# A one-token decode block rewritten on one core: 512-column score matmuls, row-form softmax and LayerNorm, a finer split of the last weight load

## The chip, the cores and the metric

One core of one Trainium2 (trn2) chip. The metric is the device time of one execution in microseconds (us), as the median of several runs. The span that a profile shows is about 1.8 us shorter than the device time of the same execution, so spans are compared with spans and times with times.

In this document PE is the tensor engine, PEld its weight loads, DVE the vector engine, ACT the scalar engine, POOL the GpSimd engine, and SP the sync engine, which issues all loads on one queue. The profile counts 16 DMA engines. PV is the product of the softmax weights with V, LN2 the second LayerNorm. A load lands at the last of the times that the trace has for it, 16 for every load but the small one of x. h2T, aT, hT and yT are small buffers of the kernels.

## The reference

One token goes through attention over the last 1024 cached positions and then through a GELU-gated feed-forward block, each behind a LayerNorm.

```python
# x: (1, 1, 640); 32 heads of 128; k_cache, v_cache: (1, 32, 4096, 128), last W = 1024 rows used
h  = x + attention(layernorm(x)) @ wo     # q = layernorm(x) @ wq, softmax(q k^T / sqrt(128)) v
h2 = h + (gelu(layernorm(h) @ w_gate) * (layernorm(h) @ w_up)) @ w_down    # F = 1728
```

All inputs are bf16. The core must read K and V (8.4 MB each), wq and wo (5.2 MB each) and w_gate, w_up and w_down (2.2 MB each), 33.9 MB in all, for a single row of activations.

## The kernel before

Every buffer is large enough to be loaded whole, so the sync engine issues the loads in order and waits only where memory is reused: wo goes where wq was, and the feed-forward weights where K was.

```python
def prog_sp(sp):
    dma(sp, "x", ...)                     # 1.2 KB
    # ... 5 loads of wq, 8 of K, 8 of V, 4 of wo, w_gate, w_up
    dma(sp, ("wd", 0), wd_view[:, 0:7, :], B_w_down[0:7 * 128, :]...)
    dma(sp, ("wd", 1), wd_view[:, 7:13, :], B_w_down[7 * 128:13 * 128, :]...)
    dma(sp, ("wd", 2), wd_view[0:F_LAST, 13, :], B_w_down[13 * 128:F, :])
```

The tensor engine transposes K, then uses large stationary matrices with a single moving column almost everywhere:

```python
for kk in range(KK):                      # scores: 8 per head, 256 in all
    t = pe.matmul(ps4[:, col:col + 1], lhsT=kT_sb[:, slot, kk * 128:(kk + 1) * 128],
                  rhs=qT_sb[:, h:h + 1], start=True, stop=True)
# ... softmax over [128, 32 x 8], maxima through PE transposes
for kk in range(KK):                      # PV: 8 per head, 256 in all
    t = pe.matmul(ps7[:, h:h + 1], lhsT=V_sb[:, h, kk, :], rhs=e_bf[:, col:col + 1],
                  start=(kk == 0), stop=(kk == KK - 1))
for c in range(DC):                       # wo: 5 per head, 160 in all
    t = pe.matmul(psb[c][:, 0:1], lhsT=wo_view[:, h, c * 128:(c + 1) * 128],
                  rhs=oT_sb[:, h:h + 1], start=(h == 0), stop=(h == H - 1))
# ... LN2 by a matmul with ones, gate and up 70 each, down 70, then:
#     h2T = down + h (DVE, 5 columns), 5 transposes to a row, copy (ACT), output load
```

## Time and profile before

| | value | view |
|---|---|---|
| time | 99.78 us (99.71 to 100.0) | runs |
| span | 98.1 us | page |
| PE and PEld instructions | 1318 + 1318 | page, part 1 |
| load rate, 22 to 58 us | 385 GB/s | stretches |
| last large w_down piece lands | 93.42 us | chain of waits |
| from there to the end | 4.7 us | chain of waits |

The page of the kernel before. The line of PE counts busy time, share of the span and instructions of each engine. The rows PEclk, DMA and GB/s have 40 slices of 2.45 us: tenths of the granted clock, tenths of busy DMA engines (9 is 90% or more), and the rate. The q1 and q8 lines are DMA queues with packets, MB and share of the 16 engines' time.

```profile
span 98.1 us, 2805 instructions
...
PE 50.2 (51%) x1318; PEld 47.6 (48%) x1318; DVE 22.0 (22%) x61; ACT 22.9 (23%) x28; POOL 1.4 (1%) x11
...
PEclk9999999999999999999965555555555555555555
DMA  3899999999999999999999999999999999998200
GB/s 47 331 421 427 427 424 373 387 386 382 386 381 388 388 381 387 381 387 387 383 386 392 376 384 365 362 364 362 363 369 397 406 403 408 377 361 284 71 0 1
...
q1 hardware_dynamic: 16420, 33.90, 93.5%
q8 instruction: 10, 0.16, 0.7%
```

The PEclk row says nothing before 26 us: the trace's first record of the clock is at 25.9 us, and the transposes before it took 0.88 us per eight, against 0.47 after it. What raised the clock there is not shown.

The DMA row is full from the third slice to the 36th, so the loads bound the kernel.

The waits of the kernel before: engine and line, whom it waited for, us in total, number of times, longest.

```profile
PE psbank L297 <- DMA wq_sb<-in_A_wo_dram: 9.8, 4, 2.7
...
PE psbank L314 <- DMA K_sb<-in_B_w_up_dram: 4.5, 1, 4.5
...
PE psbank L288 <- DMA V_sb<-in_A_v_cache_dram: 4.2, 3, 1.7
...
PE psbank L322 <- DMA K_sb<-in_B_w_down_dram: 2.7, 2, 1.7
```

In the stages behind K the tensor engine is waiting for weights and V. The end of the chain of waits, with start in us and length in us:

```profile
73.70 19.73 DMA K_sb<-in_B_w_down_dram
...
93.47 1.20 PE psbank L322 x35
...
95.16 0.71 PE psbank L327 x5
...
95.89 0.69 ACT out_row L449
```

The 35 down matmuls can start only when the second w_down piece has landed at 93.42 us. Everything after it is serial. The stretches around that landing: per microsecond, busy time of each engine, then the granted clock, the mean busy share of the 16 DMA engines, and GB/s.

```profile
core 0: us, PE busy (x) PEld busy (x) DVE busy (x) ACT busy (x) POOL busy (x), PEclk, DMA share, GB/s
...
91.00:92.00 1.00, 0.73 (x28) 0.65 (x25) 0.00 (x0) 0.00 (x0) 0.00 (x0) 0.50 0.37 112
92.00:93.00 1.00, 0.00 (x0) 0.00 (x0) 0.00 (x0) 0.00 (x0) 0.00 (x0) 0.50 0.06 20
```

### The profile page before, as it was taken

To read this page: it belongs to the slowest core of one execution; us is meant where nothing else is said; L and a number is where in the kernel's file an instruction comes from. 1 tells how busy PE (TensorE), PEld (TensorE's weight loads), DVE (VectorE), ACT (ScalarE), POOL (GpSimd) and SP (SyncE) were. 2 spreads that over 40 slices of the span, in tenths; PEclk is the share of its full clock that TensorE was granted. 3 is DMA by queue.
4 is the path that set the end of the run, shared out by engine and by line. 5 is a ranking of instruction groups with operands and counts; after the bars stand their busy time and mean duration, and the time that the engine had idled before them with its cause. 6 is when DMAs were issued, how large, how long until landed. Compare 5 with 4: busy or idle time off the path is not lost.

```text
span 98.1 us, 2805 instructions
## 1 busy us (share of the span) xinstructions
PE 50.2 (51%) x1318; PEld 47.6 (48%) x1318; DVE 22.0 (22%) x61; ACT 22.9 (23%) x28; POOL 1.4 (1%) x11
## 2 busy tenths in 40 slices
PE   0003004999999969957189353142253308036360
PEld 0002004999999969956089252142143307035360
DVE  1421000024475735732630000000000511300010
ACT  7970000004356546617060000000000070000002
POOL 5000000000000000000000000000000000000000
PEclk9999999999999999999965555555555555555555
DMA  3899999999999999999999999999999999998200
GB/s 47 331 421 427 427 424 373 387 386 382 386 381 388 388 381 387 381 387 387 383 386 392 376 384 365 362 364 362 363 369 397 406 403 408 377 361 284 71 0 1
DMA packets 16431, 34.08 MB, mean 347 GB/s; under 512 B 482, under 2 KB 6308, under 8 KB 15780
## 3 DMA queue, kind: packets, MB, share of 16 engines
q1 hardware_dynamic: 16420, 33.90, 93.5%
q8 instruction: 10, 0.16, 0.7%
q14 instruction: 1, 0.01, 0.0%
HBM read 33.90 MB, written 0.00 MB: 345 GB/s over the span
## 4 chain that ended last, share of the span: by engine, by line
DMA 33%; PE 31%; SPq 26%; issue 3%; ACT 2%; DVE 2%; DVEq 0%
SPq L187 26%; DMA K_sb<-in_B_w_down_dram 20%; PE psbank L238 18%; DMA wq_sb<-in_A_wq_dram 13%; PE psbank L248 6%; PE psbank L266 4%; PE psbank L322 1%; ACT kT_sb L339 1%; PE psbank L327 1%; ACT out_row L449 1%; DVE m_bf L363 0%; DVE sm L373 0%; ACT e_bf L441 0%; DVE h2T L424 0%; PE psbank L282 0%
## 5 line engine op out<-in xcount | busy, mean ns | idle before, releaser
L238 PE MATMUL psbank<-ident,K_sb 128*128 128x128 bf16 x256 | 21.8, 235 | 1.9 <-issue 1.9
L337 DVE COPY kT_sb<-psbank 128x1024 bf16<-128x1024 bf16 x20 | 13.7, 691 | 23.3 <-PE psbank L238 23.3
L238 PEld LDWEIGHTS psbank<-ident,K_sb 128*128 128x128 bf16 x256 | 16.6, 105 | 2.3 <-issue 2.3
L339 ACT ACTIVATE kT_sb<-psbank 128x1024 bf16<-128x1024 bf16 x12 | 12.3, 1024 | 13.3 <-PE psbank L238 13.3
L248 PE MATMUL psbank<-qT_sb,kT_sb 128*128 128x1 bf16 x256 | 11.1, 164 | 0.6 <-ACT kT_sb L339 0.6
L248 PEld LDWEIGHTS psbank<-qT_sb,kT_sb 128*128 128x128 bf16 x256 | 9.8, 98 | 0.8 <-ACT kT_sb L339 0.7
L288 PE MATMUL psbank<-e_bf,V_sb 128*128 128x1 bf16 x256 | 7.6, 165 | 4.6 <-DMA V_sb<-in_A_v_cache_dram 4.2
L297 PE MATMUL psbank<-oT_sb,wq_sb 128*128 128x1 bf16 x160 | 4.9, 165 | 9.8 <-DMA wq_sb<-in_A_wo_dram 9.8
L288 PEld LDWEIGHTS psbank<-e_bf,V_sb 128*128 128x128 bf16 x256 | 7.3, 104 | 4.9 <-DMA V_sb<-in_A_v_cache_dram 4.4
L297 PEld LDWEIGHTS psbank<-oT_sb,wq_sb 128*128 128x128 bf16 x160 | 4.6, 104 | 10.2 <-DMA wq_sb<-in_A_wo_dram 7.3
L266 PE MATMUL psbank<-xnT,wq_sb 128*128 128x1 bf16 x160 | 5.1, 166 | 7.3 <-DMA wq_sb<-in_A_wq_dram 6.9
L266 PEld LDWEIGHTS psbank<-xnT,wq_sb 128*128 128x128 bf16 x160 | 4.7, 104 | 7.7 <-DMA wq_sb<-in_A_wq_dram 7.4
L443 ACT ACTIVATE lnS<-lnS,epsc 128x1 f32<-128x1 f32 x1 | 0.3, 295 | 27.9 <-DVE lnS L400 27.9
L314 PE MATMUL psbank<-hnT,K_sb 128*128 128x1 bf16 (+1 forms) x70 | 2.2, 167 | 4.5 <-DMA K_sb<-in_B_w_up_dram 4.5
L314 PEld LDWEIGHTS psbank<-hnT,K_sb 128*128 128x128 bf16 (+1 forms) x70 | 2.1, 107 | 4.6 <-DMA K_sb<-in_B_w_up_dram 4.6
L256 PE MATMUL psbank<-ones_bf,xn_row 1*128 1x1 bf16 x5 | 0.3, 159 | 7.6 <-DVE psbank L355 7.6
L256 PEld LDWEIGHTS psbank<-ones_bf,xn_row 1*128 1x128 bf16 x5 | 0.2, 99 | 7.5 <-issue 7.5
L307 PE MATMUL psbank<-hnT,K_sb 128*128 128x1 bf16 (+1 forms) x70 | 2.2, 167 | 3.0 <-DVE hnT L402 3.0
L385 DVE TENSOR_TENSOR hT<-psbank,xT_f 128x1 f32<-128x1 f32 x5 | 0.4, 151 | 14.5 <-PE psbank L297 14.5
L307 PEld LDWEIGHTS psbank<-hnT,K_sb 128*128 128x128 bf16 (+1 forms) x70 | 2.1, 107 | 3.1 <-DVE hnT L402 3.1
L322 PE MATMUL psbank<-aT,K_sb 128*128 128x1 bf16 (+1 forms) x70 | 2.3, 165 | 2.7 <-DMA K_sb<-in_B_w_down_dram 2.7
L322 PEld LDWEIGHTS psbank<-aT,K_sb 128*128 128x128 bf16 (+1 forms) x70 | 2.1, 104 | 2.8 <-DMA K_sb<-in_B_w_down_dram 1.8
(70 smaller groups left out, 24.0 us busy)
## 6 DMA issues: line engine op xcount, KB each, us to landing
K_sb<-in_A_k_cache_dram SPq DMA_DIRECT2D x8, 1024.0 KB, 15.6
V_sb<-in_A_v_cache_dram SPq DMA_DIRECT2D x8, 1024.0 KB, 14.4
wq_sb<-in_A_wq_dram SPq DMA_DIRECT2D x5, 1024.0 KB, 9.0
wq_sb<-in_A_wo_dram SPq DMA_DIRECT2D x4, 1280.0 KB, 14.9
K_sb<-in_B_w_gate_dram SPq DMA_DIRECT2D x1, 2160.0 KB, 16.4
K_sb<-in_B_w_up_dram SPq DMA_DIRECT2D x1, 2160.0 KB, 19.1
K_sb<-in_B_w_down_dram SPq DMA_DIRECT2D x1, 1120.0 KB, 20.0
K_sb<-in_B_w_down_dram SPq DMA_DIRECT2D x1, 960.0 KB, 19.7
```

The lines of the kernel that those rows point to most:

```text
L187: sp.dma_start(out=out_ap, in_=in_ap).then_inc(sem, 16)
L238: t = pe.transpose(psT[bank][:, kk * 128:(kk + 1) * 128], K_sb[:, h, kk, :], ident[:, :])
L248: t = pe.matmul(ps4[:, col:col + 1], lhsT=kT_sb[:, slot, kk * 128:(kk + 1) * 128], rhs=qT_sb[:, h:h + 1], start=True, stop=True)
L266: t = pe.matmul(ps4[:, QOFF + h:QOFF + h + 1], lhsT=wq_sb[:, c, h * DH:(h + 1) * DH], rhs=xnT[:, c:c + 1], start=(c == 0), stop=(c == DC - 1))
L288: t = pe.matmul(ps7[:, h:h + 1], lhsT=V_sb[:, h, kk, :], rhs=e_bf[:, col:col + 1], start=(kk == 0), stop=(kk == KK - 1))
L297: t = pe.matmul(psb[c][:, 0:1], lhsT=wo_view[:, h, c * 128:(c + 1) * 128], rhs=oT_sb[:, h:h + 1], start=(h == 0), stop=(h == H - 1))
L307: t = pe.matmul(ps6[0:m, fc:fc + 1], lhsT=wg_view[:, c, fc * 128:fc * 128 + m], rhs=hnT[:, c:c + 1], start=(c == 0), stop=(c == DC - 1))
L314: t = pe.matmul(ps7[0:m, H + fc:H + fc + 1], lhsT=wu_view[:, c, fc * 128:fc * 128 + m], rhs=hnT[:, c:c + 1], start=(c == 0), stop=(c == DC ...
L322: t = pe.matmul(psb[c][:, 1:2], lhsT=wd_view[0:m, fc, c * 128:(c + 1) * 128], rhs=aT[0:m, fc:fc + 1], start=(fc == 0), stop=(fc == FC - 1))
L327: t = pe.transpose(ps_row[:, c * 128:(c + 1) * 128], h2T[:, c:c + 1], ident[:, :])
L337: ins = eng.tensor_copy(out=kT_sb[:, slot, :], in_=psT[bank][:, :])
L339: ins = eng.activation(out=kT_sb[:, slot, :], in_=psT[bank][:, :], func=ACT.Copy)
```

## The change

The intent is to use wide matmuls where the row of activations allows it. The scores of all heads go into one [32, 1024] tile, with the query placed in one column of a zeroed 32-column stationary matrix. Softmax is then done by rows, 32 partitions wide, with its scale folded into the exponential. The wo product and LN2 are done on one row. The normalisation factor is applied after the matmuls. w_down is loaded in four pieces instead of three. PV, the transposes of K, gate, up and down keep their form.

```diff
-            for kk in range(KK):
-                col = SOFF + h * KK + kk
-                t = pe.matmul(ps4[:, col:col + 1], lhsT=kT_sb[:, slot, kk * 128:(kk + 1) * 128],
-                              rhs=qT_sb[:, h:h + 1], start=True, stop=True)
+            pe.matmul(psS0, lhsT=qmask[:, h * H:(h + 1) * H], rhs=kT_sb[:, slot, 0:512],
+                      start=(h == 0), stop=(h == H - 1))
+            t = pe.matmul(psS1, lhsT=qmask[:, h * H:(h + 1) * H], rhs=kT_sb[:, slot, 512:1024],
+                          start=(h == 0), stop=(h == H - 1))
 # ... softmax: max, exp with row sum, 8 matmuls that transpose and divide, one copy
-                for c in range(DC):
-                    t = pe.matmul(psb[c][:, 0:1], lhsT=wo_view[:, h, c * 128:(c + 1) * 128],
-                                  rhs=oT_sb[:, h:h + 1], start=(h == 0), stop=(h == H - 1))
+                pe.matmul(psA0, lhsT=oT_sb[:, h:h + 1], rhs=wo_view[:, h, 0:512],
+                          start=(h == 0), stop=(h == H - 1))
+                t = pe.matmul(psA1, lhsT=oT_sb[:, h:h + 1], rhs=wo_view[:, h, 512:D],
+                              start=(h == 0), stop=(h == H - 1))
 # ... LN2: row statistics on DVE, 5 small matmuls to columns
-            dma(sp, ("wd", 0), wd_view[:, 0:7, :], B_w_down[0:7 * 128, :]...)
-            dma(sp, ("wd", 1), wd_view[:, 7:13, :], B_w_down[7 * 128:13 * 128, :]...)
-            dma(sp, ("wd", 2), wd_view[0:F_LAST, 13, :], B_w_down[13 * 128:F, :])
+            dma(sp, ("wd", 0), wd_view[:, 0:5, :], B_w_down[0:5 * 128, :]...)
+            dma(sp, ("wd", 1), wd_view[:, 5:9, :], B_w_down[5 * 128:9 * 128, :]...)
+            dma(sp, ("wd", 2), wd_view[:, 9:13, :], B_w_down[9 * 128:13 * 128, :]...)
+            dma(sp, ("wd", 3), wd_view[0:F_LAST, 13, :], B_w_down[13 * 128:F, :])
 # ... end: five copies to yT, five transposes, and on DVE one add of the row of h
-            M("act", "out_row", act.activation(out=out_row[:, :], in_=ps_row, func=ACT.Copy))
+            M("dve", "out_row", dve.tensor_tensor(out=out_row[:, :], in0=ps_row, in1=h_rowf[:, :], op=ALU.add))
```

## The prediction

> **What bounds the kernel now.** The loads do. The page's DMA row is 9 (90% or more) from the third to the 36th of 40 slices. The load queue brings 33.9 MB; the stretches show 385 GB/s between 22 and 58 us. In the timeline the sync engine's issues are paced by the queue (V issues 27.3 to 48.9), not by compute. The tensor engine waits for data in every later stage: for wo 9.8 us in four waits, w_up 4.5, V 4.2, w_down 2.7 (waits view). The chain of waits ends: the second w_down chunk lands at 93.43; 35 down matmuls 1.20; five h2T adds to 95.12; five transposes 0.71; the out_row copy 0.69; the output DMA from 96.6; end 98.1. From 89.5 to 93.4 the DMA share is only about half (windows view): some queues finish later. The change does not touch that.
>
> **What the change does, costed.**
> 1. Scores: eight 1-column matmuls per head (chain 0.18 us) become two of 512 columns. A 128-column transpose takes 0.47/8 = 58 ns at full clock, so 512 columns are about 0.22 us (estimate), 0.43 per head. PE per head goes from 0.65 to about 0.9 us; scores end near 51 us, not 46.6.
> 2. Softmax: the chain 46.66 to 49.37 (2.7 us) becomes max over 32x1024 (about 1.2, scaled from 0.42 for 256 columns), exp 1.0 to 1.2, reciprocal, diag, eight small matmuls, copy 0.4: about 4 us. PV starts near 55 instead of 49.4. PV's 256 matmuls take 7.1 us at 27 to 29 ns, so it ends about 62.5 (before 61.7); wo lands only at 64.2.
> 3. wo: 5 matmuls of 32 ns per head become 640 columns: 0.55 us per head at the half clock granted there (128 columns took 110 ns), 0.28 at full clock. A chunk of 8 heads costs 4.4 or 2.2 us against 3.6 us between landings. [...] this trace agrees in kind (transposes 0.88 to 0.47 per eight, nearly 6 us after their start). So wo ends between 77.5 (warmed) and 82 us (cold), before 76.4.
> 4. LN2: row statistics instead of ones-matmul and small ops; Exp's 1.28 us table load stays, and PE waits for rstd before the gate. w_up should land at 87.5 again, so aT stays near 90 (91 if wo is cold), ahead of the last w_down landing.
> 5. Fewer instructions, less instruction fetch: 0.1 us at most.
> 6. w_down 7/6/1 becomes 5/4/4/1: 25 matmuls instead of 35 after the last landing, 0.85 instead of 1.2: gain 0.35.
> 7. Tail: five copies for five adds (equal); the final add on the vector engine with a 640-wide row: 0.75 against 0.69: loss 0.05 to 0.1.
>
> **On the critical path:** only items 5 to 7. Predicted 99.5 us, range 98.7 to 100.6. Chances: faster 0.04, same 0.88, slower 0.08.
>
> **What would show it.** last w_down landing within 0.4 us of 93.4; scores group about 215 ns each at full clock; softmax end near 55; wo group's busy time 8 to 17 us instead of 4.9; wait for w_up still 2 to 5 us; after the last landing 4.3 us, not 4.7.
>
> **What would make it wrong.** If M=32 scores do not keep the clock up, heads cost 1.8 us and everything slides past the loads: 105 us or more. If the uneven finish of the DMA queues shrinks, up to 3 us faster.

The transposes of the kernel before started at 20.35 us and went from 0.88 to 0.47 us per eight at 26.24. Item 5 takes off up to 0.1 us and item 6 0.35, item 7 adds 0.05 to 0.1, which brings 99.78 to 99.4 to 99.5, and 99.5 was predicted. The two ends of wo in item 3 are estimates from 110 ns for 128 columns, at that clock and at twice it; which of them would hold was not shown. Four times the 58 ns of item 1 are 0.23 us, near its estimates of 0.22 us and 215 ns. That 32 rows of output (M=32) might not keep the clock up was the author's guess, and the 0.1 us of item 5 an estimate without a working. The DMA share from 89.5 to 93.4 us, "about half", was 0.34 over that window.

## More of the kernel before

Between 92 and 93 us the share is 0.06, one sixteenth: a single DMA engine is still at work and the core waits for it. In the packed trace the 16 load packets of 1,280 bytes that start in this microsecond come one at a time, each within 4 ns of the end of the one before.

## The result, and the profile after

The kernel after takes 98.24 us (98.18 to 98.32, 8 runs) against 99.78. The ratio is 0.9843, 95% interval 0.9834 to 0.9852. Ratios in this document are the mean time of one kernel's fast runs over the mean of the other's fast runs of the same rounds, so they are not quite the ratios of the medians quoted. The gain of 1.5 us is inside the predicted class (within 2%), but below the predicted range, which began at 98.7.

The page of the kernel after, the same lines:

```profile
span 96.3 us, 2243 instructions
...
PE 64.9 (67%) x1037; PEld 45.5 (47%) x1037; DVE 23.5 (24%) x56; ACT 20.5 (21%) x26; POOL 2.3 (2%) x12
...
PEclk9999999999999999999999985555589998555555
DMA  1899999999999999999999999999999999999600
GB/s 28 330 419 429 436 429 385 383 390 385 386 385 385 388 385 390 385 387 383 388 387 388 380 387 374 362 358 362 368 358 386 409 405 403 397 370 358 212 0 4
...
q1 hardware_dynamic: 16436, 33.90, 94.9%
q8 instruction: 8, 0.13, 0.6%
q14 instruction: 1, 0.01, 0.0%
```

The rate in the bulk of the run is the same. What differs is the end of the DMA row (9, 6 instead of 9, 8, 2), fewer PE instructions, and eight instruction packets in q8 instead of ten. The tensor engine's busy time went up from 50.2 to 64.9 us and cost nothing, as the chain of waits shows. Its end in the kernel after:

```profile
78.94 12.79 DMA K_sb<-in_B_w_down_dram
...
91.77 0.27 PE psbank L347 x4
...
93.20 0.71 PE psS L352 x5
...
93.93 0.81 DVE out_row L438
```

The last large piece of w_down landed at 91.73 us instead of 93.42. From there to the end it is 4.6 us, before 4.7 (predicted 4.3). So the gain is almost wholly an earlier landing, of the same bytes over the same queue. The stretches of the kernel after, columns as before:

```profile
...
91.00:92.00 1.00, 0.23 (x8) 0.23 (x9) 0.00 (x0) 0.00 (x0) 0.00 (x0) 0.50 0.16 55
92.00:93.00 1.00, 0.69 (x23) 0.59 (x20) 0.27 (x4) 0.00 (x0) 0.00 (x0) 0.50 0.00 0
...
```

The single DMA engine that worked on alone until past 93 us is gone.

The trace says more. In both programs each load raises a semaphore, a counter, by 16; the trace has 16 separate times for every load but that of x, which has two. The times don't name an engine. They are taken here as one for each of the 16 DMA engines, which agrees with the share of 0.06 from 92 to 93 us: one of the 16 times of the second w_down piece was still to come then, and from 92.3 us on one of those of the last piece. Here are these times for the late loads, in us, sorted, with the starts of the instruction packets. They are read from the packed trace, as no view of the profile prints them:

```
before                16 landings
wo, last piece        73.1 73.1 73.1 73.1 73.4 73.4 73.4 73.6 | 74.9 74.9 74.9 75.0 75.0 75.0 75.1 75.1
w_gate                78.6 78.6 78.6 78.6 78.8 78.9 78.9 79.1 | 80.4 80.4 80.5 80.5 80.5 80.5 80.6 80.6
w_up                  84.0 84.0 84.0 84.1 84.3 84.3 84.3 84.5 | 85.8 85.9 85.9 85.9 85.9 86.0 86.0 | 87.4
w_down, 2nd piece     89.8 89.8 89.9 89.9 90.1 90.1 90.1 90.3 | 91.6 91.7 91.7 91.7 91.8 91.8 91.8 | 93.4
instruction packets   21.3 27.7 34.0 40.2 46.7 53.9 60.2 72.3 84.5 91.5
after
w_up                  84.1 84.2 84.2 84.2 84.3 84.4 84.4 84.4 84.4 84.4 | 85.7 85.7 85.8 85.8 85.9 85.9
w_down, 3rd piece     89.9 90.1 90.1 90.3 90.3 90.3 90.3 90.3 90.4 | 91.5 91.6 91.6 91.6 91.6 91.7 91.7
instruction packets   21.2 27.5 40.1 52.3 63.0 69.6 86.0 89.7
```

The bars are mine. The 16 engines fall into steps about 1.4 us apart. Before the first instruction packet, all 16 land a load within 0.5 us of each other. In the kernel before, the K load that lands next after the packet at 21.3 us has one engine at 25.4 while the others are at 23.6 to 24.1; after eight packets, eight engines are late. The ninth packet, at 84.5 us, hits an engine a second time, though eight engines are still on time: one of the eight late engines falls back a second step, to 87.4, and keeps that lag until the last load. In the kernel after the loads end before a ninth packet; its eighth, at 89.7 us, came so late that it left no mark, and seven engines are late in the end.

The page calls q8 a queue of instructions, and its packets go with the tensor engine's stream: they are of 16,384 bytes, and there are ten with 2636 instructions of PE and PEld before, eight with 2074 after, and eight with 2252 in experiment 1. So they are taken as fetches of that stream, one for each whole block of instructions. The three counts then put a block between 251 and 259 instructions; here and in the expectations it is 256, an estimate (2636 / 256 = 10.3, 2074 / 256 = 8.1). The 640 memsets of experiment 6 give the same: they brought 40,960 bytes, 64 for each, and 16,384 bytes are 256 times 64. For the GpSimd engine the packets were half as large (experiment 6).

### The profile page after: what moved, and what is told of

Same layout as the page of the kernel before. It is cut to its first block, busy times and chain, and to the rows that moved or that the text cites. A ratio compares the mean times of both kernels' runs of the same rounds, so it can differ in the third digit from the quotient of the medians.

```text
span 96.3 us, 2243 instructions
## 1 busy us (share of the span) xinstructions
PE 64.9 (67%) x1037; PEld 45.5 (47%) x1037; DVE 23.5 (24%) x56; ACT 20.5 (21%) x26; POOL 2.3 (2%) x12
## 4 chain that ended last, share of the span: by engine, by line
PE 48%; DMA 26%; SPq 15%; DVE 4%; issue 3%; ACT 1%
PE psbank L254 18%; SPq L199 15%; DMA K_sb<-in_B_w_down_dram 13%; DMA wq_sb<-in_A_wq_dram 13%; PE psS L261 9%; PE psbank L305 7%; PE psS L263 7%; PE psS L281 4%; ACT E_sb L451 1%; DVE mrow L389 1%; DVE out_row L438 1%; PE psbank L347 1%; PE psS L352 1%; DVE e_sb L399 0%; DVE yT L436 0%
## 5 line engine op out<-in xcount | busy, mean ns | idle before, releaser
L364 ACT ACTIVATE kT_sb<-psbank 128x1024 bf16<-128x1024 bf16 x12 | 12.3, 1024 | 34.6 <-PE psbank L254 34.6
L254 PE MATMUL psbank<-ident,K_sb 128*128 128x128 bf16 x256 | 18.3, 230 | 0.0
L261 PE MATMUL psS<-kT_sb,qmask 128*32 128x512 bf16 x32 | 12.3, 384 | 0.0
L263 PE MATMUL psS<-kT_sb,qmask 128*32 128x512 bf16 x32 | 12.1, 379 | 0.0
L281 PE MATMUL psS<-xcT,wq_sb 128*128 128x1 bf16 x160 | 5.0, 165 | 9.7 <-DMA wq_sb<-in_A_wq_dram 9.7
L314 PE MATMUL psbank<-wq_sb,oT_sb 128*1 128x512 bf16 x32 | 10.9, 441 | 0.3 <-ACT oT_sb L456 0.3
L281 PEld LDWEIGHTS psS<-xcT,wq_sb 128*128 128x128 bf16 x160 | 4.7, 104 | 10.1 <-DMA wq_sb<-in_A_wq_dram 9.5
L305 PE MATMUL psbank<-e_sb,V_sb 128*128 128x1 bf16 x256 | 7.1, 165 | 2.7 <-issue 2.1
L305 PEld LDWEIGHTS psbank<-e_sb,V_sb 128*128 128x128 bf16 x256 | 7.0, 104 | 2.8 <-issue 2.2
L316 PE MATMUL psbank<-wq_sb,oT_sb 128*1 128x128 bf16 x32 | 7.7, 241 | 0.0
L314 PEld LDWEIGHTS psbank<-wq_sb,oT_sb 128*1 128x1 bf16 x32 | 3.0, 94 | 5.8 <-issue 2.4
L261 PEld LDWEIGHTS psS<-kT_sb,qmask 128*32 128x32 bf16 x32 | 3.0, 95 | 3.7 <-ACT kT_sb L364 0.2
L263 PEld LDWEIGHTS psS<-kT_sb,qmask 128*32 128x32 bf16 x32 | 3.1, 96 | 1.9
```

Of the source, the lines that this page charges most:

```text
L254: t = pe.transpose(psT[bank][:, kk * 128:(kk + 1) * 128], K_sb[:, h, kk, :], ident[:, :])
L261: pe.matmul(psS0, lhsT=qmask[:, h * H:(h + 1) * H], rhs=kT_sb[:, slot, 0:512], start=(h == 0), stop=(h == H - 1))
L263: t = pe.matmul(psS1, lhsT=qmask[:, h * H:(h + 1) * H], rhs=kT_sb[:, slot, 512:1024], start=(h == 0), stop=(h == H - 1))
L281: t = pe.matmul(ps_q[:, h:h + 1], lhsT=wq_sb[:, c, h * DH:(h + 1) * DH], rhs=xcT[:, c:c + 1], start=(c == 0), stop=(c == DC - 1))
L305: t = pe.matmul(ps_o[:, h:h + 1], lhsT=V_sb[:, h, kk, :], rhs=e_sb[:, col:col + 1], start=(kk == 0), stop=(kk == KK - 1))
L314: pe.matmul(psA0, lhsT=oT_sb[:, h:h + 1], rhs=wo_view[:, h, 0:512], start=(h == 0), stop=(h == H - 1))
```

## The experiments

Five theories stood against one another over the runs. They are named by letters in the expectations.

- F: the 562 instructions fewer save two block fetches. A fetch delays the loads on one DMA engine, and what counts is the engine delayed most often.
- S: the finer split of w_down moved the last landing.
- R: the row-form LN2, wo and scores shortened the path.
- L: as F, but the time falls in proportion to the instructions.
- V: it is the work or the reads that count, not the instructions.

### 1. The kernel before, a quarter of PV

Undoes nothing of the old code and only takes matmuls out of the kernel before, in a stage with slack.

```diff
-                for kk in range(KK):
+                for kk in range(2):
                     col = h * KK + kk
                     t = pe.matmul(ps7[:, h:h + 1], lhsT=V_sb[:, h, kk, :], rhs=e_bf[:, col:col + 1],
-                                  start=(kk == 0), stop=(kk == KK - 1))
+                                  start=(kk == 0), stop=(kk == 1))
```

> The kernel before, with only 2 of the 8 PV matmuls per head (a wrong result on purpose); everything else, w_down's 7/6/1 split included, as before. 192 PE matmuls fewer, with their weight loads 384 instructions. Theory F (instruction fetches): 8 or 9 packets in the instruction queue instead of 10, none of them a second delay of one DMA engine before the loads end, so the last large w_down chunk lands near 92.0 us instead of 93.4 and the time falls by 1.2 to 1.6 us, to about 98.4. Theory S (the gain came from the w_down split) and theory R (it came from the row-form LN2, wo and scores): PV has slack in front of wo, so the time stays at 99.8 within 0.2.

Measured: 98.50 us (98.43 to 98.70) against 99.77, ratio 0.9878 (0.9864 to 0.9892). The result is computed from a quarter of V; the comparison with the reference passed all the same, so it doesn't see this error. From the page of this run, instructions by engine and the instruction queue:

```profile
PE 45.1 (47%) x1126; PEld 42.5 (44%) x1126; DVE 22.0 (23%) x61; ACT 22.9 (24%) x28; POOL 1.4 (1%) x11
...
q8 instruction: 8, 0.13, 0.6%
```

Its stretches by microsecond, columns as before:

```profile
...
92.00:93.00 1.00, 0.90 (x31) 0.89 (x32) 0.00 (x0) 0.00 (x0) 0.00 (x0) 0.50 0.00 0
...
```

And its chain of waits around the last large landing, start and length in us ("issue" is time in which the engine waited for nothing that the profile shows):

```profile
73.66 18.39 DMA K_sb<-in_B_w_down_dram
92.05 0.05 issue
92.10 1.20 PE psbank L322 x35
```

There are eight instruction packets, no lone engine (share 0.00 from 92 to 93 us), and the second w_down piece (still of six blocks of 128 rows) lands at 92.05 instead of 93.42. None of the changed code is in this kernel. F holds; S and R expected 99.8.

### 2. The same with the instructions put back

This is the control for theory V: 6 dummy matmuls on a constant stand in for the 6 that were removed per head.

```diff
+                for _ in range(6):
+                    pe.matmul(psb[0][:, 200:201], lhsT=ones_bf[:, :], rhs=ones_bf[:, 0:1],
+                              start=True, stop=True)
```

> The kernel before with 2 of 8 PV matmuls per head, as in the run with a quarter of PV, but with 6 dummy 1-column matmuls per head on a constant in place of the 6 removed: the instruction count is that of the kernel before again, the reads of V are not. Theory F (instruction blocks): 10 instruction packets, one engine delayed twice, last large w_down chunk at 93.3 to 93.6, time 99.8 within 0.3. Rival theory V (the quarter of PV was faster because it read less of V or did less work): 98.5 within 0.3.

Measured: 99.74 us (99.53 to 99.79) against 99.78, ratio 0.9995 (0.9982 to 1.0008). From its page, instructions by engine and the instruction queue:

```profile
PE 50.0 (51%) x1318; PEld 47.2 (48%) x1318; DVE 22.1 (23%) x61; ACT 22.9 (23%) x28; POOL 1.4 (1%) x11
...
q8 instruction: 10, 0.16, 0.7%
```

Its chain of waits around the landing:

```profile
73.60 19.64 DMA K_sb<-in_B_w_down_dram
93.24 0.05 issue
93.28 1.20 PE psbank L325 x35
```

Ten packets, and the landing is back at 93.24. Reading less of V is worth nothing here; the instruction count is worth 1.2 us. The dummies also put the tensor engine's busy time back (45.1 to 50.0 us), but that is not what counts: the kernel after is busier, 64.9 us, and faster, and experiment 6 adds nothing to the tensor engine.

### 3. The split of w_down, alone and taken back

The kernel before with the pieces 5/4/4/1 of the diff above, and the kernel after with 7/6/1.

> The kernel before with w_down split 5/4/4/1 instead of 7/6/1, nothing else. Theory F: still 10 instruction packets and one DMA engine delayed twice; 10 matmuls fewer after the last landing, so 0.2 to 0.4 us faster, about 99.5. Theory S: the last landing moves to 91.7 and the time falls by about 1.5 us, to 98.3. Theory R: within 0.2 of before.

> The kernel after with w_down split 7/6/1 as before. Theory F: 8 instruction packets as in the kernel after, last landing stays near 91.7, 10 matmuls more after it: 0.2 to 0.4 us slower than the kernel after, about 98.5. Theory S: back to 99.8. Theory R: within 0.2 of 98.2.

Measured: the kernel before with the finer split 99.46 us, ratio to before 0.9974 (0.9962 to 0.9986), ten packets, last large landing at 93.26. The kernel after with the coarse split 98.48 us, ratio to before 0.9875 (0.9862 to 0.9887), eight packets, landing at 91.90. The chains of waits around the landing, first of the kernel before with the finer split, then of the kernel after with the coarse one:

```profile
79.19 14.07 DMA K_sb<-in_B_w_down_dram
...
93.31 0.93 PE psbank L323 x25
```

```profile
73.69 18.22 DMA K_sb<-in_B_w_down_dram
...
91.95 0.27 PE psbank L346 x4
```

So the split is worth 0.2 to 0.3 us in either kernel and doesn't decide the landing; S falls. The second run also leaves nothing for R: with the split taken back, the whole rest of the change gives 98.48 us, and the kernel before with 384 instructions fewer, the same split and eight packets too, gave 98.50.

### 4. The kernel after with instructions added early

```diff
                 for c in range(DC):
+                    if h == 0 and c > 0:
+                        for _ in range(64):
+                            pe.matmul(psb[3][:, 200:201], lhsT=ones_bf[:, :], rhs=ones_bf[:, 0:1],
+                                      start=True, stop=True)
                     Wt("pe", ("wq", c))
```

> The kernel after, with 256 dummy 1-column matmuls (512 instructions with their weight loads) put into the waits for the wq chunks, 64 in each of four waits of 2.3 us, about 1.7 us of work each. Theory F: back to 10 instruction packets, one DMA engine is delayed twice, the last large w_down chunk lands at 93.1 to 93.5 instead of 91.7, and the time rises by 1.2 to 1.7 us, to about 99.6. Theories S and R: the padding sits in idle time, so the time stays at 98.2 within 0.3.

Measured: 99.81 us, but scattered (99.35 to 100.69), ratio to before 1.0018 (0.9979 to 1.0058). There are ten packets, and the last two landings, 93.3 and 93.5, are where F puts them. The time does not prove F, though, for the tensor engine had become late itself. The chain of waits of this run in the down product:

```profile
91.59 0.27 PE psbank L351 x4
...
92.42 1.12 issue
93.53 0.27 PE psbank L351 x4
```

It began the down product at 91.6 instead of 88.6 us, and then stood for 1.12 us without a wait that the profile shows, a good microsecond after an instruction packet had started at 91.1. The padding was not free: the scores ended 4.4 us later than in the kernel after. The landing agrees with F; as a timing this run is inconclusive.

### 5. One block added late

64 dummy matmuls in front of the LN2 matmuls and 64 in front of the up matmuls, to leave the tensor engine on time.

> The kernel after with 128 dummy 1-column matmuls (256 instructions, one block) put late, 64 in the LN2 wait and 64 in the wait for w_up, so that the tensor engine is not made late as by the early padding. Theory F: a ninth instruction packet near 90 us or before falls on an engine already delayed; last w_down landings at 93.0 to 93.5 instead of 91.7 to 92.0 and 99.2 to 99.8 us. If the ninth block falls on another engine or after the loads: 98.2 to 98.5.

Measured: 98.70 us, again scattered (98.22 to 99.34), ratio to before 0.9898 (0.9866 to 0.9929). In the profiled execution (98.57) the ninth packet started at 92.7 us, after the loads, and the landings stayed at 91.8 and 92.0. The ninth block came too late to test what it was meant to, so the expected 99.2 to 99.8 was missed. Nor did the run leave the tensor engine on time: its chain runs not through the landing but through the down product, where the tensor engine stood for 1.42 us from 90.20 us without a wait that the profile shows, after the packet at 89.2. What sets the slower runs apart is not shown.

### 6. Instructions added on another engine

```diff
+        ppad = es.enter_context(nc.sbuf_tensor([128, 640], FP32))
 # ... in prog_pool:
+            for i in range(640):
+                pool.memset(ppad[:, i:i + 1], 1.0)
```

> The kernel after with 640 one-column memsets on the otherwise idle GpSimd engine (2.5 blocks of 256 instructions), early in the run. If fetches of any engine's instructions delay DMA engines in the same way: 2 to 3 packets more in the instruction queue, and, if they fall on engines that the tensor engine's fetches also meet, the last landing 1.4 us later and the time 99.6; if they fall on others, 98.2 within 0.3. If only the tensor engine's stream matters, no more packets and 98.2 within 0.3.

Measured: 99.85 us (99.76 to 99.93), ratio to before 1.0002 (0.9983 to 1.0020): the whole gain is gone. Its chain of waits around the last large landing:

```profile
80.63 12.78 DMA K_sb<-in_B_w_down_dram
93.41 0.04 issue
93.45 0.27 PE psbank L350 x4
```

One microsecond of its stretches, columns as before:

```profile
...
92.00:93.00 1.00, 0.36 (x14) 0.27 (x11) 0.00 (x0) 0.00 (x0) 0.00 (x0) 0.50 0.07 23
...
```

And the instruction queues of its page:

```profile
q8 instruction: 8, 0.13, 0.6%
q14 instruction: 6, 0.05, 0.1%
```

The large w_down piece lands at 93.41, with one engine alone at the end, and the chain runs through that landing, not through a late tensor engine, which waited for it for a microsecond. q8 still shows eight packets, but q14, which has one in the kernel after, has six. The trace gives the five new ones: 8,192 bytes each, at 7.2, 12.1, 16.9, 22.0 and 27.1 us; the GpSimd engine ran the memsets from 2.9 to 25.9 us. Five times 8,192 bytes are 64 for each of the 640 memsets, as 16,384 bytes for 256 instructions are. That is the 40 KB of the expected 2.5 blocks, in smaller packets. The landings show what they did: the last of a load's 16 was 0.2 us behind the sixth before the first packet, then 0.5 us at 8.8 us, 1.2 at 14.4, 1.9 at 20.3, 2.6 at 23.7 and 3.2 at 29.7, a step for each packet, and stayed 3.3 us behind afterwards. The landings don't name their engine, but a lag that adds up like this is that of a single one. So instructions of another engine delay the loads in the same way, here all five packets on one DMA engine, by 0.6 to 0.7 us for each packet after the first. This is the clearest run for F: the tensor engine's stream and packet count are those of the kernel after.

### 7. The kernel after, a quarter of PV

The edit of experiment 1 in the kernel after: does taking out more instructions give more?

> The kernel after with only 2 of 8 PV matmuls per head (a wrong result on purpose): 384 instructions fewer. Theory F, as a step (what counts is the engine delayed most often, and one delay remains): 6 or 7 instruction packets, last landing still near 91.7, time 98.2 within 0.3. Rival theory L (the time follows the amount of instruction bytes or instructions): a further 0.8 to 1.1 us faster, since 562 fewer gave 1.5.

Measured: 98.38 us (98.17 to 98.44), ratio to before 0.9849 (0.9828 to 0.9871), that of the kernel after being 0.9843. There are six packets, five late engines instead of six or seven, and the last large landing is at 91.80. L expected 97.1 to 97.4 and falls. The gain is a step: it is had when no engine is delayed twice, and five late engines instead of six or seven bring nothing, as one late engine is enough to hold the load: in experiment 6 one alone held it until 93.41 us. A kernel with no late engine at all was not tried.

### 8. Towards a faster version

Two edits on the kernel after: w_down in pieces 5/4/2/2/1, and on top of that the small load of x behind the first wq load. The second is shown.

```diff
-            dma(sp, "x", x_row[:, :], A_x[0, :, :])
             for c in range(DC):
                 dma(sp, ("wq", c), wq_sb[:, c, :], A_wq[c * 128:(c + 1) * 128, :])
+                if c == 0:
+                    dma(sp, "x", x_row[:, :], A_x[0, :, :])
```

> The kernel after with w_down split 5/4/2/2/1 instead of 5/4/4/1. All theories: the last landings stay near 91.7 to 92.0; 15 instead of 25 matmuls remain after the last but one, so 0.2 to 0.45 us faster than the kernel after, 97.8 to 98.0.

> As the run with the 5/4/2/2/1 split, and the small load of x is issued after the first wq load instead of before it, so that every large load starts about 0.4 us sooner (the x issue takes 0.34 us of the sync engine before the first wq issue at 1.1). If the load stream decides the end, 0.3 to 0.45 us faster than the run with the split alone, 97.4 to 97.6; if the start of the loads is set by something else, no difference.

Measured: 98.00 us (97.76 to 98.24), ratio to before 0.9817 (0.9795 to 0.9839), and 97.73 us (97.58 to 97.94), ratio 0.9789 (0.9766 to 0.9813). The second is the fastest version found, about 0.5 us below the kernel after (0.9789 against 0.9843 of before). Its step of 0.27 us over the first is just under the expected 0.3 to 0.45, and the two intervals overlap, so the sign is likely and the size not settled. Its last landing in the chain is at 91.83, in the first at 92.13.

## Why the prediction was wrong

- **What bounds the kernel: right.** The loads did, before and after. 15 us more of busy tensor engine cost nothing.
- **Scores (1): cost right, end late.** 0.22 us each at full clock, as predicted (the granted clock was 1.00 from 23 to 52.7 us); the scores ended at 52.7 us (predicted about 51).
- **Softmax and PV (2): chain right, PV late.** Softmax took 4.1 us (52.76 to 56.89) and PV started at 56.9 us (predicted 55). PV ended at 66.2 instead of 62.5: 1.9 us of this are the later start, and 2.1 us are a time in which the tensor engine stood still. The chain of waits of the kernel after shows it:

```profile
56.93 6.49 PE psbank L305 x238
63.42 2.13 issue
65.56 0.65 PE psbank L305 x18
```

"issue" is time without a wait that the profile shows. It starts just after the instruction packet at 63.0 us, so the likely cause is the same fetch, seen from the other side; this is not shown. It had slack and cost nothing: the chain goes on through the loads.

- **wo (3): right.** It ended at 77.4 us (predicted 77.5 if the clock rose). It did: the wo matmuls went from 0.53 to 0.27 us per head at 70.7 us, 4.2 us after their start, and the granted clock from 0.50 to 1.00. What raised it is not shown.
- **LN2 (4): order right, times early.** The wait for w_up was 1.8 us, not 2 to 5, as w_up landed at 85.9, not 87.5; that landing too had waited for the engine delayed twice (87.4 in the kernel before, the other 15 by 86.0).
- **Split and tail (6, 7): right in size.** The split gave 0.2 to 0.3 us (predicted 0.35), and the last add took 0.81 us against 0.69 for the copy (loss 0.12, predicted 0.05 to 0.1). After the landing 4.6 us were left, not 4.3.
- **Fewer instructions (5): the step that failed.** The prediction said "0.1 us at most". It measured 1.2 us: the ratio 0.9878 in experiment 1 is 1.22 us less than 99.77, in a kernel where nothing else that matters changed. So the landing, which was to stay within 0.4 us of 93.4, came at 91.73. The prediction gives no working; 33 KB at the 385 GB/s of all 16 DMA engines would be 0.09 us (an estimate from the two figures), which fits its number. But the down product waited for the last of the 16 engines (93.42 us, the other 15 by 91.8), and a block falls on one engine (one more was late after each of the first eight packets). The two packets saved are 33 KB out of 34 MB, and one of them was the second delay of one engine.
- **"The change does not touch that."** The prediction saw the uneven finish from 89.5 to 93.4 us and named its shrinking as what could make it wrong ("up to 3 us faster"), but didn't ask what made it uneven. The numbers were at hand: q8 listed ten packets, and a share of 0.06 at 92 us is one engine.

The sum closes: 1.22 us for the instructions and 0.26 us for the split (0.9974 x 99.77) make 1.48 of the 1.57 us that the ratio 0.9843 stands for.

Left open: which engine a block falls on. In the four traces of the tensor engine's ten blocks (the kernel before, with the finer split, with the dummies, and with early padding) the first eight blocks delayed eight different engines and the ninth one of these, though eight others were on time; what rule there is behind this is not shown, and the five packets of the GpSimd engine all fell on one engine. Why a block of 16 KB costs 1.4 us is also open, where one engine's share of the load, 385/16 = 24 GB/s, would move it in 0.7 us (an estimate from these figures). The packets of 8 KB in experiment 6 cost 0.6 to 0.7 us each, about half as much.

## What to carry to other kernels

In a kernel bound by loads, look at the last microseconds of the DMA share: here a sixteenth (0.06 from 92 to 93 us) was one straggling engine, and two packets of 16,384 bytes, one of them the second on that engine, cost the whole core 1.2 us out of 33.9 MB of loads (experiment 1). The long unrolled stream of tiny matmuls had a price even in idle time, for there was one such packet among the loads for about 256 instructions of the tensor engine (ten for 2636, eight for 2074). Count the packets of every engine, since the gain came in a step here (eight packets 98.24 us, six 98.38, ten 99.78), and read all the lines of instruction queues on the page: the five packets that cost 1.6 us in experiment 6 were in q14, not in q8. And when a prediction says that something ends unevenly, find out why before calling it untouched.
